# Warm-up matmuls on four 32-column tiles, and a last output piece of 128 columns, in a GeGLU feed-forward kernel

## The chip, the cores and the metric

The kernel runs on one core of a Trainium2 chip. The metric is the device time of one execution, in microseconds. Each run would be called slow if it were over 1.5% above the fastest run of the same kernel. Before the change the median of the first three runs was 300.06 us (299.55 to 300.38).

The *span* is the time from the first to the last instruction of the profiled execution. The device time is longer than the span; in the first profile the two were 299.16 and 297.38 us.

## The reference

```python
B, S, D, F = 32, 32, 1024, 3584          # x: 1024 tokens of 1024, bf16, all weights bf16
def reference(x, w_gate, w_up, w_down):
    return (gelu(x @ w_gate) * (x @ w_up)) @ w_down      # gelu: tanh approximation
```

## The kernel before

In the profile, PE is the tensor engine and PEld its weight loads, DVE the vector engine, ACT the scalar engine, POOL the GpSimd engine and SP the engine that issues most of the DMAs; a q after a name (PEq, SPq) is that engine's instruction queue. PSUM (`ps`) is the memory that the tensor engine writes its products to; to *evict* a result is to copy it from there.

Every operation is recorded with the buffers that it reads and writes; semaphore waits follow from that. One helper line emits nearly all of them, so almost every line of the profile says L98, and groups are told apart by their tiles. (L163 is a second emitter, for matmuls that keep the weights of the matmul before.)

The head. `ident` is an identity matrix. The eight constant matmuls compute nothing that is used. Two pieces of x are loaded as they are (`xn`) and transposed on the tensor engine, so that the first columns of x are there sooner than the transposing DMAs bring the rest (in the profile before, the first of those landed at 7.60 us).

```python
one = nc.const_aps.tensor(1.0, [P, 512], BF16)
# ... ident is built on POOL ...
for n in [512] * 6 + [128] * 2:
    pr.add("pe", "matmul", ps[:, 3, 0:n], one[:, 0:P], one[:, 0:n], start=True, stop=True, w=[("ps", 3)])

NX = 2
for i, eng in enumerate(("sp", "act")):
    pr.add(eng, "dma_start", xn[:, 2 * i:2 * i + 2, :], x_r[:, 2 * i:2 * i + 2, 0:NX * P], w=[("xn", i)], dma=f"xn{i}")
# ... loads of the first weights, transposing loads of the rest of x ...
for k in range(NX):
    for i, b in enumerate((6, 7) if k == 0 else (4, 5)):
        half = ps[:, b, 0:P].bitcast(BF16)
        for t in range(2):
            pr.add("pe", "transpose", half[:, t * P:(t + 1) * P], xn[:, 2 * i + t, k * P:(k + 1) * P],
                   ident[:, :], r=[("xn", i), "ident"], w=[("ps", b)])
        pr.add("dve", "tensor_copy", xT[:, k, i * 256:(i + 1) * 256], half, r=[("ps", b)], ...)
```

The middle is a dense stream of 128x512 products (`xT` with `wg` and `wu`, then `hT` with `wd`), with a gelu on ACT and a product on DVE for each tile. It is not changed. The end:

```python
jobs = [[(tc, 0, 512), (tc, 512, 512)] for tc in range(TC - 1)]
jobs += [[(TC - 1, 0, 512)], [(TC - 1, 512, 256)], [(TC - 1, 768, 256)]]
for job in jobs:
    # ... 28 matmuls for each piece of the job, accumulated in one PSUM bank ...
    for tc, col, n in job:
        # eviction on ACT or DVE in turn, then one DMA of the piece to the output
```

The kernel ends with a wait on SP for the last output DMA.

## Time and profile before

| | before |
|---|---|
| median of six runs | 299.99 us (299.55 to 300.54) |
| tensor engine (PE) busy | 98% of the span |
| first real product | 4.61 us |
| last eviction starts | 294.96 us |
| end of the span | 297.38 us |

The first lines are from the page of the kernel before: busy time and share by engine, the engines and lines of the chain that ended last, and two groups (busy time, mean ns of one, then the idle time just before them).

```profile
PE 292.7 (98%) x1362; PEld 79.3 (27%) x808; DVE 42.5 (14%) x68; ACT 37.5 (13%) x67; POOL 0.7 (0%) x6
...
PE 98%; issue 0%; ACT 0%
PE ps L98 56%; PE ps L163 43%; ACT xT L98 0%
...
L98 PE MATMUL ps<-const-bfloat16-1.0 128*128 128x512 bf16 (+1 forms) x8 | 2.9, 545 | 0.8 <-PEq L309 0.8
...
L98 PEld LDWEIGHTS ps<-ident,xn 128*128 128x128 bf16 x8 | 0.8, 136 | 0.0
```

The chain is the tensor engine from end to end, so work on any other engine is hidden unless it comes before the first product or after the last one. The last line, with 0.0 us idle before the transposes' weight loads, says that x had come by the time the constant matmuls were done.

The timeline of the tensor engine in the head and of ACT later, of the same kernel; columns are start, duration of the merged group, what it was, and the idle time before it:

```profile
0.78 2.93 PE L98 MATMUL ps<-const-bfloat16-1.0 128*128 128x512 bf16 x8 [0.78 <-PEq L309]
3.51 1.06 PE L98 MATMUL ps<-ident,xn 128*128 128x128 bf16 x8
4.61 1.02 PE L98 MATMUL ps<-xT,wg 128*128 128x512 bf16 x4
...
15.60 0.60 ACT L98 ACTIVATE g<-ps 128x512 f32<-128x512 f32 x1 [10.58 <-PE ps L98]
...
294.96 0.38 ACT L98 ACTIVATE xT<-ps 128x256 bf16<-128x256 f32 x1 [5.52 <-PE ps L98]
295.37 0.33 SPq L98 DMA_DIRECT2D out_dram<-xT  x1
```

A matmul's recorded duration can be longer than the distance to the next one's start (0.631 and 0.427 us for the constant matmuls), so the distance between starts is what counts. Those distances are read from the trace's single records, which the views merge. Six constant matmuls are 0.427 us apart (the first two 0.381), two of 128 columns 0.107 us, the transposes 0.107 us; then the four products on `wg` are 0.215 us apart. The clock therefore doubled between the transposes and the first product, and the trace's clock record agrees: full clock from 4.591 us. The two pieces of `xn` landed at 3.40 and 3.62 us by the semaphore records, just as the constant matmuls ended.

### The profile page before, as it was taken

The numbers are of one execution on the slowest core, as the hardware profiler recorded it, in microseconds if no ns is written. First come the engines' busy times: TensorE is split into PE (matmuls) and PEld (weight loads), VectorE is DVE, ScalarE is ACT, GpSimd is POOL, SyncE is SP. The second block draws the span as 40 slices with busy tenths as digits, with TensorE's granted clock in tenths as the row PEclk, the third lists the DMA queues.
The fourth block names the chain that finished last, engine by engine and source line by source line (L and its number), as shares of the span: only waits on it lengthen the run. The fifth ranks groups of instructions, "written<-read, shape, count | busy, mean of one in ns | idle before, by whom it ended". The sixth has DMA issues, their size and how long they took to land.

```text
span 297.4 us, 2549 instructions
## 1 busy us (share of the span) xinstructions
PE 292.7 (98%) x1362; PEld 79.3 (27%) x808; DVE 42.5 (14%) x68; ACT 37.5 (13%) x67; POOL 0.7 (0%) x6
## 2 busy tenths in 40 slices
PE   8999999999999999999999999999999999999996
PEld 4444222222222222222222222222222222222255
DVE  1030311112211111111111221110000000000000
ACT  1030411111111111211111111110000000000010
POOL 0000000000000000000000000000000000000000
PEclk9999999999999999999999999999999999999999
DMA  7999734006608309121030030000101101001011
GB/s 201 268 247 354 237 106 142 1 0 225 198 2 304 121 10 355 62 102 39 0 141 2 0 141 0 0 2 0 35 0 37 35 0 35 15 23 35 0 35 35
DMA packets 28842, 26.37 MB, mean 89 GB/s; under 512 B 8224, under 2 KB 25248, under 8 KB 28832
## 3 DMA queue, kind: packets, MB, share of 16 engines
q1 hardware_dynamic: 26640, 24.25, 25.5%
q10 hardware_dynamic: 2192, 1.97, 2.3%
q8 instruction: 8, 0.13, 0.2%
q14 instruction: 2, 0.02, 0.0%
HBM read 22.28 MB, written 2.10 MB: 82 GB/s over the span
## 4 chain that ended last, share of the span: by engine, by line
PE 98%; issue 0%; ACT 0%
PE ps L98 56%; PE ps L163 43%; ACT xT L98 0%
## 5 line engine op out<-in xcount | busy, mean ns | idle before, releaser
L98 PE MATMUL ps<-xT,wg 128*128 128x512 bf16 x250 | 88.4, 379 | 0.3
L98 PE MATMUL ps<-xT,wu 128*128 128x512 bf16 x250 | 87.9, 379 | 0.2
L98 PE MATMUL ps<-wd,hT 128*128 128x512 bf16 (+1 forms) x272 | 83.6, 357 | 0.0
L163 PE MATMUL ps<-wd,hT 128*128 128x512 bf16 x196 | 74.3, 379 | 0.4
L163 PE MATMUL ps<-xT,wu 128*128 128x512 bf16 x189 | 71.6, 379 | 0.3
L163 PE MATMUL ps<-xT,wg 128*128 128x512 bf16 x189 | 71.6, 379 | 0.2
L98 DVE TENSOR_TENSOR hT<-g,ps 128x512 bf16<-128x512 f32 x56 | 36.3, 685 | 158.1 <-PE ps L98 152.5
L98 ACT ACTIVATE g<-ps 128x512 f32<-128x512 f32 x56 | 30.8, 595 | 159.8 <-PE ps L98 159.8
L98 PEld LDWEIGHTS ps<-wd,hT 128*128 128x128 bf16 x280 | 27.4, 98 | 69.8 <-issue 65.8
L98 PEld LDWEIGHTS ps<-xT,wu 128*128 128x128 bf16 x256 | 25.0, 98 | 71.7 <-issue 64.1
L98 PEld LDWEIGHTS ps<-xT,wg 128*128 128x128 bf16 x256 | 25.0, 98 | 71.5 <-issue 64.0
L98 DVE CAST xT<-ps 128x512 bf16<-128x512 f32 (+1 forms) x8 | 5.3, 658 | 87.7 <-ACT xT L98 79.8
L98 ACT ACTIVATE xT<-ps 128x512 bf16<-128x512 f32 (+1 forms) x9 | 5.2, 573 | 94.6 <-PE ps L98 94.6
L98 PE MATMUL ps<-const-bfloat16-1.0 128*128 128x512 bf16 (+1 forms) x8 | 2.9, 545 | 0.8 <-PEq L309 0.8
L98 ACT ACT_TABLE_LOAD x1 | 1.3, 1283 | 3.5 <-issue 3.5
L98 PEld LDWEIGHTS ps<-const-bfloat16-1.0 128*128 128x128 bf16 x8 | 1.0, 137 | 2.4 <-issue 2.4
L98 DVE COPY xT<-ps 128x256 bf16<-128x256 bf16 x4 | 0.9, 292 | 4.0 <-PE ps L98 4.0
L98 PE MATMUL ps<-ident,xn 128*128 128x128 bf16 x8 | 1.1, 311 | 0.0
L98 PEld LDWEIGHTS ps<-ident,xn 128*128 128x128 bf16 x8 | 0.8, 136 | 0.0
L98 POOL TENSOR_SCALAR_AFFINE_SELECT ident<-ident 128x128 bf16<-128x128 bf16 x1 | 0.3, 295 | 0.2 <-POOL ident L98 0.2
L98 POOL MEMSET ident<- 128x128 bf16 x1 | 0.2, 205 | 0.3 <-POOLq L309 0.3
L98 ACT ACTIVATE warm<-const-float32-0.0 128x1 f32<-128x1 f32 x1 | 0.2, 203 | 0.0
(4 smaller groups left out, 0.4 us busy)
## 6 DMA issues: line engine op xcount, KB each, us to landing
wd<-in_w_down_dram SPq DMA_DIRECT2D x7, 1024.0 KB, 5.1
wg<-in_w_gate_dram SPq DMA_DIRECT2D x6, 1024.0 KB, 7.8
wu<-in_w_up_dram SPq DMA_DIRECT2D x6, 1024.0 KB, 10.1
out_dram<-xT SPq DMA_DIRECT2D x15, 128.0 KB, 1.7
wg<-in_w_gate_dram ACTq DMA_DIRECT2D x3, 256.0 KB, 4.9
wu<-in_w_up_dram ACTq DMA_DIRECT2D x3, 256.0 KB, 5.2
wu<-in_w_up_dram ACTq DMA_DIRECT2D x2, 128.0 KB, 3.8
wg<-in_w_gate_dram SPq DMA_DIRECT2D x2, 128.0 KB, 3.3
```

The source lines that it names most:

```text
L98: ins = name(eng, *args, **kw) if callable(name) else getattr(eng, name)(*args, **kw)
L163: return eng.add_instruction(mybir.InstMatmult(start_tensor_calc=start, stop_tensor_calc=stop, ldweights=False, name=nc.get_next_instructi ...
```

## The change

The intent: do the warm-up with matmuls that use the four 32-column tiles of the array at once (24 of them, in six rounds of four), and make the piece of work that is exposed at the very end smaller. The Trainium skill, "TensorEngine Tiling (Array Packing)", Key Properties, says that tiles operate independently and that a change of the tiling mode drains the engine.

```diff
-        for n in [512] * 6 + [128] * 2:
-            pr.add("pe", "matmul", ps[:, 3, 0:n], one[:, 0:P], one[:, 0:n], start=True, stop=True, w=[("ps", 3)])
+        for i in range(24):
+            j = 32 * (i % 4)
+            pr.add("pe", "matmul", ps[j:j + 32, 3, :], one[:, 0:32], one[:, :], start=True, stop=True, w=[("ps", 3)])
@@
-        jobs += [[(TC - 1, 0, 512)], [(TC - 1, 512, 256)], [(TC - 1, 768, 256)]]
+        jobs += [[(TC - 1, 0, 512)], [(TC - 1, 512, 384)], [(TC - 1, 896, 128)]]
```

## The prediction

> **What bounds the kernel now.** The tensor engine: busy 98% of the 297.4 us span (busy table; the chain that ended last is 98% PE). From the first real product at 4.61 us the timeline shows a 512-column matmul every 0.215 us without holes, so only the first 4.6 us and the end can change.
>
> - Head (timeline). Six constant matmuls of 512 columns start 0.427 us apart and two of 128 columns 0.107 us apart, from 0.78 to 3.51 us: half clock. Eight transposes follow, also half clock, then copies by DVE, and the first product at 4.61 us, the first thing at full clock. So the head warms the clock and fills the wait for two pieces of x: issued at 0.74 us, landing 2.7 and 2.9 us later, about 3.4 to 3.6 us.
> - Tail (timeline). The last matmuls of 256 columns run 0.109 us apart; the last eviction on ACT starts at 294.96 us and takes 0.384 us; its DMA is issued at 295.37 us and lands 1.6 us later.
>
> **The change, costed.**
> 1. Head. 24 matmuls with 32 output columns, four tiles of the array in turn. If the four run together, six rounds of 0.427 us = 2.56 us instead of 2.73. The Trainium skill, "TensorEngine Tiling (Array Packing)", Key Properties, says that tiles run independently and that a change of tiling mode drains the engine. No run here shows either yet. The drain costs perhaps 0.2 us (a matmul's recorded 0.63 us less its 0.427 us interval; my estimate). The saving is off the critical path: the transposes cannot start before x lands. Expected: 0 us, -0.05 to +0.2.
> 2. Clock. If four tiles count as more activity, full clock might come before 4.6 us; then eight transposes save up to 8 x 0.053 = 0.4 us. If they count as less, it comes a window later ("TensorE: Matmul & The Clock Gate", Part 1: 3.4 us; here 3.8 us from first matmul to full clock), costing about 1.7 us. I expect no move: first product within 0.2 us of 4.61.
> 3. Tail. The last two pieces keep their columns (384+128 against 256+256): 6.1 us at the present rate, if a 128-column matmul (0.056 us) still hides its weight load[...]. The last eviction shrinks from 0.384 to about 0.28 us (597 ns for 512 columns: 0.83 ns a column). A DMA of half the size lands perhaps 0.03 us sooner. The 384-column piece is evicted and sent under the last matmuls. Gain about 0.13 us, all on the path after PE.
>
> Sum: -0.1 to -0.2 us, under the spread of the three runs (299.55 to 300.38).
>
> **Predicted: 299.8 us, 298.9 to 301.2 us in 8 of 10. Faster by over 2%: 0.01; within 2%: 0.96; slower by over 2%: 0.03.**
>
> **What would show each step.** Head: constant matmuls in groups of four starting close together, groups 0.43 us apart, transposes near 3.5 us. Clock: first products 0.215 us apart, starting near 4.6 us. Tail: 128-column matmuls 0.056 us apart; last eviction about 0.28 us; the time from last matmul to end shorter by 0.1 us.
>
> **What would make it wrong.** Tiles running one after the other: nine at half clock until 4.6 us and fifteen at 0.215 us, transposes at about 7.9 us, some 4 us late (+1.3%); if the clock does not rise either, 24 x 0.427 = 10.2 us, over 7 us late. An earlier clock gives up to 0.5 us, but later loads of x and the weights may take part of it back.

## The result, and the profile after

The changed kernel took 299.90 us (median of six runs, 299.15 to 300.04); the kernel before took 299.99 us in the same rounds (six runs, 299.55 to 300.54). The ratio is 0.999, with a 95% interval from 0.9975 to 1.0006. Here and below a ratio is the mean time of one kernel's fast runs over that of the other's in the same rounds, so it is not quite the ratio of the medians.

The same lines of the page of the kernel after:

```profile
PE 294.4 (99%) x1404; PEld 77.8 (26%) x824; DVE 42.7 (14%) x68; ACT 37.4 (13%) x67; POOL 0.7 (0%) x6
...
PE 96%; DMA 2%; SPq 0%; issue 0%; ACT 0%
PE ps L98 54%; PE ps L163 42%; DMA xT<-in_x_dram 2%; SPq L98 0%; ACT xT L98 0%
...
L98 PE MATMUL ps<-const-bfloat16-1.0 128*32 128x512 bf16 x24 | 2.8, 627 | 0.8 <-PEq L310 0.8
...
L98 PEld LDWEIGHTS ps<-ident,xn 128*128 128x128 bf16 x8 | 0.7, 132 | 1.1 <-DMA xn<-in_x_dram 1.0
```

The rise from 98% to 99% means nothing: 1362 matmuls were recorded before and 1404 after, and some records are missing from each. Two things do mean something. The 24 tiled matmuls cost 2.8 us together, as much as eight full ones. And the transposes' weight loads, whose operand is `xn`, now wait for the DMA that brings it (`xn<-in_x_dram`). The chain also has a DMA in it now, a load of x (`xT<-in_x_dram`).

The timeline of the kernel after, the same places:

```profile
0.78 2.75 PE L98 MATMUL ps<-const-bfloat16-1.0 128*32 128x512 bf16 x24 [0.78 <-PEq L310]
3.62 1.05 PE L98 MATMUL ps<-ident,xn 128*128 128x128 bf16 x8
4.72 1.15 PE L98 MATMUL ps<-xT,wg 128*128 128x512 bf16 x4
...
8.65 1.02 PE L98 MATMUL ps<-xT,wg 128*128 128x512 bf16 x4 [0.19 <-DMA xT<-in_x_dram]
...
16.23 0.60 ACT L98 ACTIVATE g<-ps 128x512 f32<-128x512 f32 x1 [11.19 <-PE ps L98]
...
295.59 0.28 ACT L98 ACTIVATE xT<-ps 128x128 bf16<-128x128 f32 x1 [5.52 <-PE ps L98]
295.89 0.33 SPq L98 DMA_DIRECT2D out_dram<-xT  x1
```

In this one execution the first gelu came 0.63 us later than before (16.23 against 15.60), and the end came 0.39 us later (297.77 against 297.38). The difference between those two numbers, 0.24 us, is the gain of the tail. From the trace's records:

| stretch | before | after |
|---|---|---|
| start to first gelu | 15.601 us | 16.230 us |
| first gelu to last gelu | 179.420 us | 179.419 us |
| last gelu to last eviction | 99.938 us | 99.939 us |
| last eviction to end | 2.420 us | 2.181 us |

The middle is equal to 1 ns, though its last part is cut 384 + 128 instead of 256 + 256. So there are two questions. Is the later first gelu the work of the change, or chance? And is the tail's gain real in the times?

Ahead of the first gelu, three things differed. x landed at 3.57 and 3.81 us instead of 3.40 and 3.62. The full clock came at 5.001 us instead of 4.591. And a later load of x held the products up: one distance between starts was 0.569 us instead of 0.216 (the view above shows only 0.19 us of it as idle, since the recorded duration of the matmul before covers the rest).

### The profile page after: what moved, and what is told of

It reads as the page before. It is cut to its first block, busy times and chain, and to the rows that moved or that the text cites. A ratio compares the mean times of both kernels' runs of the same rounds, so it can differ in the third digit from the quotient of the medians.

```text
span 297.8 us, 2607 instructions
## 1 busy us (share of the span) xinstructions
PE 294.4 (99%) x1404; PEld 77.8 (26%) x824; DVE 42.7 (14%) x68; ACT 37.4 (13%) x67; POOL 0.7 (0%) x6
## 3 DMA queue, kind: packets, MB, share of 16 engines
q10 hardware_dynamic: 2192, 1.97, 2.5%
## 4 chain that ended last, share of the span: by engine, by line
PE 96%; DMA 2%; SPq 0%; issue 0%; ACT 0%
PE ps L98 54%; PE ps L163 42%; DMA xT<-in_x_dram 2%; SPq L98 0%; ACT xT L98 0%
## 5 line engine op out<-in xcount | busy, mean ns | idle before, releaser
L98 PE MATMUL ps<-xT,wg 128*128 128x512 bf16 x256 | 90.3, 379 | 0.2 <-DMA xT<-in_x_dram 0.2
L98 PE MATMUL ps<-xT,wu 128*128 128x512 bf16 x256 | 90.2, 379 | 0.0
L98 PE MATMUL ps<-wd,hT 128*128 128x512 bf16 (+2 forms) x280 | 86.6, 358 | 0.0
L163 PE MATMUL ps<-xT,wg 128*128 128x512 bf16 x192 | 72.8, 379 | 0.0
L163 PE MATMUL ps<-xT,wu 128*128 128x512 bf16 x192 | 72.8, 379 | 0.0
L98 PEld LDWEIGHTS ps<-wd,hT 128*128 128x128 bf16 x280 | 26.3, 98 | 71.0 <-issue 65.8
L98 PE MATMUL ps<-const-bfloat16-1.0 128*32 128x512 bf16 x24 | 2.8, 627 | 0.8 <-PEq L310 0.8
L98 PEld LDWEIGHTS ps<-const-bfloat16-1.0 128*32 128x32 bf16 x24 | 0.9, 134 | 1.7 <-issue 1.7
```

The costliest lines, as they stand in the source:

```text
L98: ins = name(eng, *args, **kw) if callable(name) else getattr(eng, name)(*args, **kw)
L163: return eng.add_instruction(mybir.InstMatmult(start_tensor_calc=start, stop_tensor_calc=stop, ldweights=False, name=nc.get_next_instructi ...
```

## The experiments

Theory: the head change does nothing (its saving lies in front of a wait for x), the tail gains 0.24 us, and all of it drowns in the differences from run to run, which come from when the full clock is granted and when x lands. Rival A: the head change costs time, which cancels the tail's gain. Rival B: the tensor engine gives the tail's gain back. All kernels below gave correct results.

### The two halves: head_only and tail_only

`head_only` has the new head and the old end; `tail_only` the other way round:

```diff
@@ head_only, against the kernel before
-for n in [512] * 6 + [128] * 2: ...
+for i in range(24): ...            # as in the change
@@ tail_only, against the kernel before
-[(TC - 1, 512, 256)], [(TC - 1, 768, 256)]
+[(TC - 1, 512, 384)], [(TC - 1, 896, 128)]
```

> The head of the change alone; the last piece keeps 256 columns. Theory (the head saves 0.17 us of matmul time, but the transposes wait for x, so nothing reaches the end): ratio to the kernel before 1.000, within 0.001. Profile: constant matmuls in six groups of four, groups 0.427 us apart, ending about 3.3 us; the transposes' start follows the landing of x (3.4 to 3.8 us). Rival A (the head costs time, by the drain and the idle stretch before the transposes, and cancels a gain of the tail): ratio 1.0005 to 1.002, the full clock granted later than 4.6 us in this run too.

> The last piece of 128 columns alone, with the old head. Theory: 0.24 us faster (2.42 us from the start of the last eviction to the end in the profile before, 2.18 in the profile after): ratio 0.999 to 0.9995; eviction about 277 ns, issue to landing about 1.48 us against 1.61. Rival A says the same here and a loss in the head alone. Rival B (the tail's gain is given back by the tensor engine, whose 384- and 128-column matmuls take longer than two times 256): the stretch from the first matmul of the last two pieces to the last eviction longer than 6.30 us, ratio 1.000.

Measured, against 299.85 us for the kernel before (median of 11 runs, 299.24 to 300.34): head_only 300.15 us (ratio 1.0011, interval 0.9998 to 1.0025), tail_only 300.02 us (ratio 1.0008, interval 0.9994 to 1.0023). Neither is told from 1, and tail_only's ratio missed what I expected, with the sign reversed. head_only's ratio lies just outside what the theory allowed (1.000, within 0.001) and inside rival A's range (1.0005 to 1.002), but its interval covers both. The traces say more. The time from last eviction to end was 2.401 us in head_only and 2.189 us in tail_only, so that gain goes with the last piece. The full clock came at 6.364 and at 6.323 us. The first is late, as rival A said; but the second has the old head, so a late clock needs no tiled head. From first gelu to last eviction both took the same as the two first profiles within 2 ns, which rules out rival B. Rival A stays possible after this pair.

### Are the tiles what makes the matmuls run together? one_tile

```diff
-            j = 32 * (i % 4)
+            j = 0
```

> The changed kernel with all 24 constant matmuls on the first tile of 32 columns. If it is the use of four tiles that makes them run together: now one after the other, 0.427 us apart at half clock and 0.215 us at full clock. The transposes then start at about 7 to 8 us if the full clock comes at about 4.6 to 5 us (kernel 3.5 to 4.5 us slower, ratio 1.012 to 1.015), and at about 11 us (ratio 1.025) if one tile in four is too little activity to raise the clock. If narrow matmuls were short for another reason, the time stays at ratio 1.000.

It took 303.09 us, ratio 1.011 (1.0094 to 1.0126). Its tensor engine's timeline:

```profile
0.77 7.46 PE L98 MATMUL ps<-const-bfloat16-1.0 128*32 128x512 bf16 x24 [0.77 <-PEq L310]
8.17 0.62 PE L98 MATMUL ps<-ident,xn 128*128 128x128 bf16 x8
```

The 24 matmuls on one tile follow one another and last until about 8.1 us, against 3.3 us on four tiles. The median is 3.24 us above the kernel before, a little under the 3.5 to 4.5 us that I expected: I had compared it with a kernel whose products always start at full clock, and the kernel before often has a few at half clock, as will be seen. In the kernel after, the four of a round start within 0.03 us, and the rounds are 0.427 us apart: four at the price of one. In one_tile the clock came at 5.046 us, so a quarter of the array is activity enough to raise it.

### What the constant matmuls are for: no_head and head_12

```diff
@@ no_head, against the kernel before
-for n in [512] * 6 + [128] * 2:
-    pr.add("pe", "matmul", ps[:, 3, 0:n], ...)
@@ head_12, against the kernel after
-for i in range(24):
+for i in range(12):
```

> The kernel before without any constant matmul. Transposes still wait for x and start at 3.4 to 3.8 us, so the start of the first product stays near 4.6 us; the full clock, if it takes one whole window of about 3.4 us of activity, comes 3 to 6.8 us after the first transpose. Products run 0.427 us apart until then: each us at half clock costs half a us, so 1 to 3 us slower, ratio 1.003 to 1.010. If instead the clock does not depend on the constant matmuls, ratio 1.000.

> The changed kernel with 12 constant matmuls on tiles (three rounds) instead of 24. They end at about 2.1 us; the tensor engine then idles until x lands at 3.4 to 3.7 us. Theory (the clock is raised at the end of a 3.413 us window that was mostly busy; windows 63 to 71% busy did not raise it in three profiles, one some 82% busy did): no window before the transposes can be busy enough, so the full clock comes after 6.5 us, as without a head; about 0.9 us slower than before (ratio 1.003), transposes still starting 0.05 us after x lands. Rival (any matmuls before x lands are enough to start the count, so half the head does as well): ratio 1.000 and a full clock at 4.2 to 6.4 us.

no_head took 300.71 us (ratio 1.0031, interval 1.0014 to 1.0047) against 299.85. head_12 took 300.49 us against 300.11 in its rounds (ratio 1.0019, interval 0.9999 to 1.004). The ratio of head_12 is less than I expected and its interval just reaches 1; its trace fits the theory. The timelines of the tensor engine, no_head first:

```profile
3.32 1.09 PE L98 MATMUL ps<-ident,xn 128*128 128x128 bf16 x8 [3.32 <-DMA xn<-in_x_dram]
4.46 1.86 PE L98 MATMUL ps<-xT,wg 128*128 128x512 bf16 x4
6.12 1.71 PE L98 MATMUL ps<-xT,wu 128*128 128x512 bf16 x4
```

and head_12:

```profile
0.77 1.47 PE L98 MATMUL ps<-const-bfloat16-1.0 128*32 128x512 bf16 x12 [0.77 <-PEq L310]
3.23 1.04 PE L98 MATMUL ps<-ident,xn 128*128 128x128 bf16 x8 [0.98 <-DMA xn<-in_x_dram]
4.32 1.86 PE L98 MATMUL ps<-xT,wg 128*128 128x512 bf16 x4
5.98 1.91 PE L98 MATMUL ps<-xT,wu 128*128 128x512 bf16 x4
7.69 1.25 PE L98 MATMUL ps<-xT,wg 128*128 128x512 bf16 x4
8.77 1.03 PE L98 MATMUL ps<-xT,wu 128*128 128x512 bf16 x4
```

Four products at full clock take 1.03 us in this view, at half clock 1.9 us. The full clock came at about 8.1 us here and at about 7.5 us in no_head (read from these distances; these two traces have no clock record). The transposes started 0.046 us after x landed in both, although one had no head at all: in these two x sets their start, not the matmuls before them. What the constant matmuls buy is the clock.

### Take the clock and the loads out of the comparison: the fixed-start kernels

Here the transposes wait for a chain of eleven DVE copies of known length, while 22 constant matmuls keep the tensor engine at work. By then the full clock must have come and x must have landed. The kernel is slower on purpose. Four versions differ only in the end:

```diff
-        for n in [512] * 6 + [128] * 2: ...
+        pr.add("pe", "matmul", ps[:, 0, :], one[:, 0:P], one[:, :], start=True, stop=True, w=[("ps", 0)])
+        for n in range(21):
+            pr.add("pe", "matmul", ps[:, 3, :], one[:, 0:P], one[:, :], start=True, stop=True, w=[("ps", 3)])
+        for n in range(11):
+            c = 512 * (n % 2)
+            pr.add("dve", "tensor_copy", wd[:, n // 2, c:c + 512], ps[:, 0, :], r=[("ps", 0)], w=["delay", ("wd", n // 2)])
@@ transposes
-   r=[("xn", i), "ident"]
+   r=[("xn", i), "ident", "delay"]
@@ the end: fixed_256 as before; fixed_128 as after; then
+   fixed_64:  [(TC - 1, 512, 448)], [(TC - 1, 960, 64)]
+   fixed_512: [(TC - 1, 512, 512)]
```

> Slower on purpose: the old tail (256 columns), and a head in which the transposes wait for a chain of eleven copies on DVE (about 9 us by 0.66 us each) while 22 constant matmuls keep the tensor engine at work. In four profiles the full clock was granted at 4.59, 5.00, 6.32 and 6.36 us, all in steps of the same 3.413 us (293.546 us of full clock in each is 86 of them), and after the first gate activation every stretch was the same to 1 ns (179.42 us, then 99.94 us). Theory: the spread of the runs, over 1 us, is when the full clock comes, and when x lands; here both are over before the first product. So: first product at about 9.8 us, no product at half clock, no wait for x; about 304.5 us; the range of the runs under 0.4 us instead of 1.3 us. If the spread has another cause (outside the profiled span, the loads, the tail), it stays over 1 us.

> The same head with the last piece of 128 columns. Theory: with the spread gone, the gain of the tail can be seen in the times: 0.23 us (0.15 to 0.30) less than the run of the same head with 256 columns (medians), and in the profile 2.18 us from the start of the last eviction to the end against 2.41. Rival: it is given back by the tensor engine; then the two are equal within 0.1 us, and the stretch from the first gate activation's end of phase to the last eviction is longer by 0.2 us.

> The same head with 448 and 64 columns at the end. If a 64-column matmul still goes at its columns (0.03 us each), the eviction falls to about 225 ns and the DMA a little more: 0.05 to 0.12 us faster than 128 columns. If a matmul with its own weight load cannot start more often than every 0.05 us or so, the tensor engine loses 28 times 0.02 us = 0.5 us, and it is about 0.4 us slower than 128 columns.

> The same head with one last piece of 512 columns. The doubled cost: eviction 597 ns against 384, and a DMA of 128 KB that takes 1.67 us against 1.61: about 0.27 us slower than 256 columns.

| | runs | median, range of times | last eviction | its DMA, issue to landing | last eviction to end |
|---|---|---|---|---|---|
| kernel before, same rounds | 9 | 299.84 us, 299.14 to 300.74 | | | |
| fixed_512 | 4 | 304.04 us, 304.03 to 304.06 | 0.691 us (DVE) | 1.711 us | 2.817 us |
| fixed_256 | 5 | 303.70 us, 303.69 to 303.82 | 0.383 us (ACT) | 1.611 us | 2.417 us |
| fixed_128 | 4 | 303.65 us, 303.47 to 303.68 | 0.278 us (ACT) | 1.478 us | 2.169 us |
| fixed_64 | 4 | 303.60 us, 303.57 to 303.70 | 0.223 us (ACT) | 1.489 us | 2.121 us |

**The spread is explained.** With the same chip and rounds, the range fell from 1.60 us to between 0.03 us (fixed_512) and 0.21 us (fixed_128), though over four or five runs each instead of nine. So the spread comes from ahead of the first products; these kernels take out the clock and the landing of x together, and the table further down tells them apart. The chain of copies came in shorter than I thought (copies start 0.598 us apart), so the first product came at 9.15 us instead of 9.8, and the time was 303.7 us instead of 304.5. The profile of fixed_64 is the exception that fits: its full clock came latest, at 6.614 us, so its constant matmuls outlasted the copies and its products began 0.205 us later than in the other three.

**The tail, in the profile and in the times.** The timelines of the last eviction, fixed_256 first:

```profile
299.50 0.38 ACT L98 ACTIVATE xT<-ps 128x256 bf16<-128x256 f32 x1 [5.52 <-PE ps L98]
299.91 0.33 SPq L98 DMA_DIRECT2D out_dram<-xT  x1
```

and fixed_128:

```profile
299.50 0.28 ACT L98 ACTIVATE xT<-ps 128x128 bf16<-128x128 f32 x1 [5.52 <-PE ps L98]
299.80 0.33 SPq L98 DMA_DIRECT2D out_dram<-xT  x1
```

Both evictions start at 299.50 us: the matmuls of 384 + 128 columns took as long as those of 256 + 256. The DMA is issued 0.10 us sooner, and the spans are 301.92 and 301.67 us. In the other runs, whose spans are rounded to 0.1 us, all four of fixed_128 are 301.7 and the five of fixed_256 are 301.9 to 302.0. But the device times differ by 0.05 us only, not by 0.23. Three of the four runs of fixed_128 spent 1.94 to 1.98 us outside the span, where fixed_256 spent 1.79 to 1.82 us; the fourth spent 1.77 us and took 303.47 us, which is 0.23 us under fixed_256. fixed_64 shows the same (1.97 to 2.00 us in three of four). So the shorter end is real within the span, and in most of these runs some 0.17 us of it was given back outside it. What that is, no run here shows. tail_only and tail_64 had 1.74 to 1.84 us outside, and the kernel after had 1.75 to 1.83 us in four runs and 1.94 to 1.95 us in two, so it does not always come with a small last piece.

**How far it goes.** 64 columns gain another 0.05 us from last eviction to end, all in the eviction; the DMA's time no longer falls. The tensor engine loses nothing, since 64-column matmuls start 0.029 us apart, and 128-column ones 0.056 us, each with its own weight load. fixed_512 was 0.34 us slower than fixed_256 (expected: 0.27), partly because the number of pieces also moved the last eviction to DVE, at 0.691 us.

### The combination: tail_64, and each kernel once more

tail_64 is the kernel before with 448 + 64 columns at the end. before_again and after_again are the two kernels unchanged, one look each.

```diff
-[(TC - 1, 512, 256)], [(TC - 1, 768, 256)]
+[(TC - 1, 512, 448)], [(TC - 1, 960, 64)]
```

> The combination that the runs point to: the old head, which leaves less idle time before the transposes, and a last piece of 64 columns (64-column matmuls went 0.029 us apart in the fixed-head run). From the start of the last eviction to the end 2.12 us against 2.42 before and 2.18 after; the two phases in the middle 179.42 and 99.94 us less 0.05 or so. Times: 0.1 to 0.3 us less than before, ratio 0.999 to 0.9997, which the interval will hardly tell from 1.

> The kernel before, profiled once more. If the differences between the two first profiles ahead of the first gate activation (full clock at 4.59 and 5.00 us, x landing 0.17 us later, a wait of 0.35 us for x) are chance, this one also differs from the first profile there by some tenths of a us, and after it is equal to 0.02 us: 179.42, 99.94 and 2.40 to 2.42 us.

> The kernel after, profiled once more: 179.42, 99.94 and 2.17 to 2.19 us; transposes 0.05 us after x lands; the full clock anywhere from 4.2 to 7.3 us.

tail_64 took 299.80 us (298.94 to 300.49) against 300.11 us (11 runs, 299.19 to 300.99): ratio 0.9988, interval 0.9965 to 1.0011. It has the lowest run of all and a span's end of 2.141 us, but on these runs it cannot be called faster than either kernel.

The repeated looks answer the question about the first gelu. All profiles but those of one_tile and the fixed-start kernels, from the records (us):

| profile | x landed (two pieces) | transposes start | first product | full clock from | first gelu | then to last eviction | to the end |
|---|---|---|---|---|---|---|---|
| before | 3.40, 3.62 | 3.506 | 4.612 | 4.591 | 15.60 | 279.358 | 2.420 |
| before_again | 3.58, 3.78 | 3.625 | 4.706 | 5.052 | 16.21 | 279.358 | 2.413 |
| tail_only (old head) | 3.43, 3.63 | 3.499 | 4.605 | 6.323 | 16.81 | 279.358 | 2.189 |
| tail_64 (old head) | 3.55, 3.77 | 3.594 | 4.682 | 5.222 | 16.52 | 279.358 | 2.141 |
| after | 3.57, 3.81 | 3.620 | 4.724 | 5.001 | 16.23 | 279.358 | 2.181 |
| after_again | 3.16, 3.34 | 3.456 | 4.538 | 4.918 | 16.49 | 279.358 | 2.184 |
| head_only | 3.69, 3.95 | 3.736 | 4.864 | 6.364 | 16.58 | 279.358 | 2.401 |
| no_head | 3.28, 3.54 | 3.323 | 4.460 | about 7.5 | 16.93 | 279.358 | 2.398 |
| head_12 | 3.18, 3.41 | 3.230 | 4.323 | about 8.1 | 17.18 | 279.358 | 2.179 |

The kernel before, unchanged, had its first gelu at 15.60 us in one execution and at 16.21 us in another, with nearly the same clock time and landing of x as the kernel after had. So the 0.63 us between the two first profiles is within what the kernel before does by itself. The lines of before_again, its first gelu and its wait on the tensor engine:

```profile
16.21 0.60 ACT L98 ACTIVATE g<-ps 128x512 f32<-128x512 f32 x1 [11.20 <-PE ps L98]
...
PE ps L98 <- DMA wg<-in_w_gate_dram: 0.2, 1, 0.2
```

The kernel after_again, with the earliest x of all full heads, still reached the first gelu late, because it then waited longer for a later load of x, as its waits show (engine and line, what was waited for, total us, times, longest):

```profile
PE ps L98 <- PEq L310: 0.8, 1, 0.8
PE ps L98 <- DMA xT<-in_x_dram: 0.6, 1, 0.6
```

The records also tell the clock and the loads apart. From the first product to the first gelu it is 10.99 us in the first profile of the kernel before, in one_tile and in all four fixed-start kernels, where no product ran at half clock and none waited long for a load. What the others took beyond that is, within 0.05 us, the sum of two parts: half the time from the first product to the full clock (a product at half clock takes twice as long), and the gaps between starts in which a load was waited for, less the usual 0.216 us (a single gap of 0.432 us is a missing record). In head_only, no_head and head_12 it is the clock (0.73, 1.48 and 1.87 us beyond; half the time is 0.75, 1.52 and 1.89 us). In before_again, after, after_again and tail_64 the longest gap gives most of it (0.34, 0.35, 0.72 and 0.60 of 0.51, 0.52, 0.97 and 0.85 us). In tail_only it is both (0.86 and 0.37 of 1.22 us).

## Why the prediction was right

**Head: 0 us expected, -0.05 to +0.2.** The four tiles ran together, six rounds 0.427 us apart, as the prediction's main case had it; one_tile shows the other case, 3 us slower. In the profile after and in head_only the saving was hidden by the landing of x: the transposes started 0.047 and 0.046 us after it. In after_again x was early, and there the head itself was the limit: its last round would have ended at 3.319 us, and the transposes started at 3.456 us, not 0.05 us after x as I had expected. The 0.14 us between is the cost of leaving the tiling mode, as the skill's page on tiling says there would be (it gives no figure; I had estimated 0.2 us). In one_tile it was 0.10 us. After full-width constant matmuls there is no such gap: in fixed_64, also at full clock, the transposes started 0.220 us after the last of them, in one_tile 0.312 us. With the old head, transposes started at 3.50 us at the earliest (before and tail_only). So the new head can save about 0.05 us, and only when x lands before about 3.4 us.

**Clock: no move expected, first product within 0.2 us of 4.61.** The first product came at 4.72 and 4.54 us (after and after_again), so that half was right; with the same head and the latest x it came at 4.86 us (head_only). The other half, that the products run at full clock from the start, was true of the first profile only (one_tile and the fixed-start kernels, slower by design, apart): the full clock came anywhere from 4.59 to 6.61 us in the twelve profiles that have the record, with old and new heads. I read one profile's 3.8 us from first matmul to full clock as a constant. It differs from run to run, with no edit to the kernel (4.591 and 5.052 us for the kernel before). The length of the full-clock stretch was 293.546 us in seven profiles and 296.960 us in the other five: 86 and 87 times 3.4133 us. That fits a fixed grid of windows, whose place against the start of the kernel differs from run to run; the skill, "TensorE: Matmul & The Clock Gate", Part 1, says just that (a free-running window of 3413 ns). It also moves the time: until the full clock comes, each product takes 0.427 us instead of 0.215.

**Tail: 0.13 us expected, 0.24 us measured in the span.** The parts were the eviction, expected to fall from 0.384 to about 0.28 us and measured at 0.277, and the DMA, expected 0.03 us sooner and measured 0.13 us sooner (1.610 to 1.478 us). The DMA is the term that was too small: I had only the rounded 1.6 and 1.7 us for 64 and 128 KB to go by. The matmuls kept their time exactly, 0.0558 us apart at 128 columns. The 384-column piece was sent under the last matmuls, as foreseen.

**Sum.** -0.1 to -0.2 us was predicted, and the medians differ by 0.09 us, within an interval that includes 0. The agreement of that number is partly luck; what the runs support is a gain of about 0.24 us at the end of the span, and a head whose effect is too small to be seen.

**Still open.** Rival A in a weak form: the new head leaves the tensor engine idle a little longer before the transposes, and a window that is not busy enough does not raise the clock. By my count from the records, in windows of 3.413 us laid back from the moment of the full clock, the window before the last was 63% (tail_only: 2.14 us busy), 64% (head_only: 2.18 us), 71% (fixed_64: 2.43 us) and about 57% busy (head_12: 1.93 us) and did not raise it. The last one, at whose end the full clock came, was about 82% busy in after (2.81 us) and about 78% in head_only (2.67 us). That window of head_only holds all the idle time of the new head before the transposes, with the latest x of all profiles, and raised the clock all the same; so that idle time can matter only in a window that lost time elsewhere too, for instance before the first matmul. Were the new head to cost 0.1 us on average that way, head_only's interval (0.9998 to 1.0025) would not exclude it. Open too is the 0.17 us outside the span in some runs with a small last piece.

## What to carry to other kernels

When the tensor engine is busy from the first product to the last, look at what comes before and after, and cost each piece against what it waits for: a shorter head in front of a load gains nothing, while the last eviction and its DMA are paid in full. To see a gain of a tenth of a per cent, compare stretches of the trace that start after the part that differs from run to run (here, from the first gelu on), or build a version in which that part is over before the work starts; here that brought the range of the runs from 1.60 us to 0.21 us or less. And take no time of an event in a single profile for a constant before a second look.

## What the Trainium skill lacked or had wrong

- "TensorE: Matmul & The Clock Gate", Back-to-back issue gap, gives about 81 ns (128 columns) and 131 ns (512 columns) for each matmul in a stream of weight load and matmul pairs. Here such pairs started 55.8 ns apart at 128 columns (fixed_128 and after) and 216 ns apart at 512; 64 and 256 columns took 29.2 and 109.2 ns. The same page's formula for a single matmul (columns over 2.4, plus 2.5 ns) fits all four, with the weight load wholly hidden.
- The same page, Part 4, says that the full clock does not engage for transposes. Here transposes started 0.107 us apart at half clock and about 0.055 us apart once the full clock had been granted (one_tile, fixed_256). By the count above they also seem to count as work: without its eight transposes (0.85 us) the window that raised the clock in head_only would be only 53% busy, less than the 71% that did not.
- "TensorEngine Tiling (Array Packing)", Key Properties, gives no cost for leaving a tiling mode: 0.10 us at full clock (one_tile), 0.14 us at half clock (after_again), counted from the end of the last round's columns to the next start.
- I found no page that says how busy a window must be to raise the clock, or whether work on a part of the array counts: 32 of 128 columns were enough (one_tile, 5.046 us); windows up to some 71% busy did not raise it (fixed_64), one of about 78% did (head_only).
- "Runtime: NRT & Kernel Launch", The ~15µs preamble/postamble breakdown, lists what runs around a kernel, but not which of it a device time like this one takes in, nor that it varies: outside the span of the instructions there were 1.74 to 2.00 us in these runs, not constant for one kernel.
